# Column-tiled attention sums per 512-token block, table Gelu and Silu, and a hand-ordered interleave with the FFN matmuls

## The chip, the cores and the metric

One core of a Trainium2 chip; the rounds ran on different chips. The metric is the device time of one execution in microseconds, as a median over several executions; lower is better. A profile adds a span, from the first to the last instruction, which in the profiled runs here lies about 2 us below the time. Engines: PE is TensorE, DVE is VectorE, ACT is ScalarE, POOL is GpSimd, SP issues transfers. A "slot" is what one full 128x128x512 matmul takes in a stream.

## The reference

```python
x = A_x                                   # (1, 2048, 512) bf16
xn = layernorm(x)
q, k, v = split_heads(xn @ wqkv)          # 32 heads of 16
# each query attends to 8 keys, at distances 0, 2, ..., 14 back
logits = q . k[pos - 2*w] / 4             # w = 0..7, masked before the start
o = softmax(logits) @ v[pos - 2*w]
s = o @ wo
g = silu((gelu_tanh(xn @ w_gate) * (xn @ w_up)) @ w_down)   # 512 -> 1792 -> 512
return x + s * g
```

## The kernel before

Features lie on partitions, tokens along the free axis. A score is a product on DVE followed by a sum over the 16 features of each head, which PE does with a 0/1 matrix. The kernel runs stage after stage over all 2,048 tokens, and a scheduler chooses the order of instructions. The parts that matter here, cut:

```python
# scores: per window position w, per 128 features c, over all tokens
nc.vector.tensor_tensor(out=prodk[:], in0=q_sb[:, c, :],
                        in1=k_sb[:, c, koff : koff + S], op=ALU.mult)
for jq in range(NJ):
    o = 32 * jq + 8 * c
    nc.tensor.matmul(L_ps[:],                                  # all 128 rows
        lhsT=ind1[:, IND1_OFF - o : IND1_OFF - o + P],         # 128 columns, 8 not zero
        rhs=prodk[:, jq * TQ : (jq + 1) * TQ], ...)
# ... softmax over [128, 8, 512] at once, on DVE and ACT ...
# values: 128 products of 512 columns, each summed by a matmul with the identity
nc.vector.tensor_tensor(out=pv[:], in0=attn[:, w, :],
                        in1=v_arr[:, d, voff : voff + TQ], op=ALU.mult)
nc.tensor.matmul(oacc_ps[:], lhsT=ident[:], rhs=pv[:], start=(w == 0), stop=(w == W - 1))
# ...
# FFN, per 128 of the 1792 hidden features ("a pair": gate and up, 4 matmuls each)
nc.scalar.activation(out=u_bf[:], in_=u_ps[:], func=AF.Copy)
nc.scalar.activation(out=zt[:], in_=g_ps[:], func=AF.Square, scale=sqrt_c2)
nc.vector.scalar_tensor_tensor(out=zt[:], in0=zt[:], scalar=c1, in1=g_ps[:], op0=ALU.add, op1=ALU.mult)
nc.scalar.activation(out=zt[:], in_=zt[:], func=AF.Tanh)
nc.vector.scalar_tensor_tensor(out=gu[:], in0=g_ps[:], scalar=0.5, in1=u_bf[:], op0=ALU.mult, op1=ALU.mult)
heng.scalar_tensor_tensor(out=hT[:, fc, :], in0=zt[:], scalar=1.0, in1=gu[:], op0=ALU.add, op1=ALU.mult)
```

The softmax here doesn't subtract the row's maximum and nothing guards it: scores larger than these inputs give would overflow.

## Time and profile before

| | before |
|---|---|
| time, median of 3 runs | 321.88 us (320.28 to 322.45) |
| span of the profiled run | 319.8 us |
| busy PE / DVE / ACT | 287.3 / 245.1 / 165.8 us |
| full matmuls x slot | 1,184 x 0.2165 = 256.3 us |

One more view belongs beside them: the chain of waits, summed by engine. Its shares are of the span, and each part names what the end of the program was waiting on.

```profile
PE 48%; DVE 30%; ACT 17%; issue 2%; DMA 1%; DVEq 0%; ACTq 0%
```

Less than half of the end's path is PE's own work; 30% is DVE and 17% ACT.

### The profile page before, as it was taken

The page shows a single profiled execution, that of the slowest core. Times are in us where ns is not written, and L with a number is a line of the kernel's source. Part 1 is how long each engine was busy: PE and PEld are TensorE (multiplying, and loading weights), DVE is VectorE, ACT ScalarE, POOL GpSimd, SP SyncE. Part 2 cuts the span into 40 slices and gives each one's busy share as a digit, 9 for nine tenths or more (in the row PEclk, how much of TensorE's full clock was granted, in tenths as well). Part 3 has the DMA queues.
Part 4 walks back from the last instruction along what each step waited for, and adds up shares of the span by engine and source line. Part 5 has one row for each costly group of instructions (what it writes and reads, how often), then busy time and mean ns, then how long its engine had stood idle before and what let it go on. Part 6 is the DMA issues. An engine that isn't in the chain of part 4 may idle for free.

```text
span 319.8 us, 3547 instructions
## 1 busy us (share of the span) xinstructions
PE 287.3 (90%) x1248; PEld 119.6 (37%) x1248; DVE 245.1 (77%) x460; ACT 165.8 (52%) x281; POOL 1.4 (0%) x10
## 2 busy tenths in 40 slices
PE   0698999999998576999999999999999999999993
PEld 0444444444433222444332343344443334443341
DVE  4867710159999699989999999944389995899954
ACT  1155986642201835622222488827558882588811
POOL 1000000000000000000000000000000000000000
PEclk9999999999999956999999999999999999999998
DMA  7997111110000093000000197102410001200012
GB/s 248 395 371 235 66 35 33 67 66 0 2 0 0 1 214 56 1 0 0 2 0 1 28 198 240 61 0 68 132 53 14 2 0 36 87 10 1 0 35 66
DMA packets 17762, 22.57 MB, mean 71 GB/s; under 512 B 1104, under 2 KB 15696, under 8 KB 17744
## 3 DMA queue, kind: packets, MB, share of 16 engines
q1 hardware_dynamic: 17744, 22.34, 23.3%
q8 instruction: 10, 0.16, 0.2%
q14 instruction: 8, 0.07, 0.1%
HBM read 16.04 MB, written 6.29 MB: 70 GB/s over the span
## 4 chain that ended last, share of the span: by engine, by line
PE 48%; DVE 30%; ACT 17%; issue 2%; DMA 1%; DVEq 0%; ACTq 0%
DVE pv L275 13%; PE qkv_ps L181 13%; PE y_ps L358 13%; PE L_ps L223 7%; ACT zt L345 7%; DVE zt L342 7%; ACT zt L341 7%; PE g_ps L322 5%; PE s_ps L304 4%; PE u_ps L331 4%; DVE prodk L215 3%; DVE stats L142 1%; ACT u_bf L339 1%; PE tr_ps L162 1%; DVE hT L351 1%
## 5 line engine op out<-in xcount | busy, mean ns | idle before, releaser
L322 PE MATMUL g_ps<-xnT,wg_sb 128*128 128x512 bf16 x224 | 61.5, 391 | 8.1 <-ACT u_bf L339 2.8
L331 PE MATMUL u_ps<-xnT,wu_sb 128*128 128x512 bf16 x224 | 60.7, 390 | 6.2 <-ACT u_bf L339 3.9
L215 DVE TENSOR_TENSOR prodk<-q_sb,k_sb 128x2048 bf16<-128x2048 bf16 x32 | 37.5, 1222 | 25.0 <-ACT k_sb L196 21.0
L358 PE MATMUL y_ps<-wd_sb,hT 128*128 128x512 bf16 x224 | 55.3, 379 | 0.6
L181 PE MATMUL qkv_ps<-xnT,wqkv_sb 128*128 128x512 bf16 x192 | 43.7, 387 | 0.0
L275 DVE TENSOR_TENSOR pv<-attn,v_arr 128x512 bf16<-128x512 bf16 x128 | 43.0, 416 | 0.0
L342 DVE SCALAR_TENSOR_TENSOR zt<-zt,g_ps 128x512 bf16<-128x512 bf16 x56 | 38.3, 684 | 5.5 <-ACT zt L341 0.7
L345 ACT ACTIVATE zt<-zt 128x512 bf16<-128x512 bf16 x56 | 35.2, 629 | 12.0 <-DVE zt L342 11.6
L281 PE MATMUL oacc_ps<-pv,ident 128*128 128x512 bf16 x128 | 41.2, 378 | 0.0
L351 DVE SCALAR_TENSOR_TENSOR hT<-zt,gu 128x512 bf16<-128x512 bf16 x56 | 38.4, 686 | 3.5 <-ACT zt L345 2.8
L339 ACT ACTIVATE u_bf<-u_ps 128x512 bf16<-128x512 f32 x56 | 33.2, 593 | 14.1 <-PE u_ps L331 13.6
L341 ACT ACTIVATE zt<-g_ps 128x512 bf16<-128x512 f32 x56 | 33.1, 596 | 13.9 <-PE g_ps L322 7.8
L347 DVE SCALAR_TENSOR_TENSOR gu<-g_ps,u_bf 128x512 bf16<-128x512 f32 x56 | 38.3, 684 | 0.2 <-ACT u_bf L339 0.2
L322 PEld LDWEIGHTS <-wg_sb 128*128 128x128 bf16 x224 | 22.1, 99 | 42.6 <-issue 22.8
L331 PEld LDWEIGHTS <-wu_sb 128*128 128x128 bf16 x224 | 22.2, 100 | 33.2 <-issue 9.3
L223 PE MATMUL L_ps<-prodk,ind 128*128 128x512 bf16 x128 | 32.6, 378 | 1.7 <-DVE prodk L215 0.9
L358 PEld LDWEIGHTS <-hT 128*128 128x128 bf16 x224 | 21.5, 97 | 29.0 <-issue 3.3
L181 PEld LDWEIGHTS <-wqkv_sb 128*128 128x128 bf16 x192 | 18.9, 100 | 21.5 <-issue 0.2
L288 ACT ACTIVATE o_arr<-oacc_ps 128x512 bf16<-128x512 f32 x16 | 9.6, 597 | 33.2 <-PE oacc_ps L281 33.2
L367 DVE SCALAR_TENSOR_TENSOR g<-th,y_ps 128x512 bf16<-128x512 bf16 x16 | 10.9, 686 | 20.3 <-ACT th L366 20.3
L366 ACT ACTIVATE th<-y_ps 128x512 bf16<-128x512 f32 x16 | 9.5, 597 | 31.0 <-PE y_ps L358 30.7
L281 PEld LDWEIGHTS <-ident 128*128 128x128 bf16 x128 | 11.7, 96 | 23.3 <-issue 9.5
(41 smaller groups left out, 153.8 us busy)
## 6 DMA issues: line engine op xcount, KB each, us to landing
x_chunk<-in_A_x_dram SPq DMA_DIRECT2D x4, 512.0 KB, 4.8
x_t<-in_A_x_dram SPq DMA_DIRECT2D x16, 128.0 KB, 2.3
vT_dram<-vst SPq DMA_DIRECT2D x16, 128.0 KB, 1.8
oT_dram<-o_arr SPq DMA_DIRECT2D x4, 512.0 KB, 7.8
oT_fm<-oT_dram SPq DMA_DIRECT2D x4, 512.0 KB, 5.2
out_dram<-o_t SPq DMA_DIRECT2D x16, 128.0 KB, 1.7
wg_sb<-in_B_w_gate_dram SPq DMA_DIRECT2D x1, 1792.0 KB, 14.7
wu_sb<-in_B_w_up_dram SPq DMA_DIRECT2D x1, 1792.0 KB, 9.2
```

Source lines behind the costliest of these rows:

```text
L181: nc.tensor.matmul(ps[:], lhsT=wqkv_sb[:, dk, fo * P : (fo + 1) * P], rhs=xnT[:, dk, jq * TQ : (jq + 1) * TQ], start=(dk == 0), stop=(dk = ...
L215: nc.vector.tensor_tensor(out=prodk[:], in0=q_sb[:, c, :], in1=k_sb[:, c, koff : koff + S], op=ALU.mult,)
L223: nc.tensor.matmul(L_ps[:], lhsT=ind1[:, IND1_OFF - o : IND1_OFF - o + P], rhs=prodk[:, jq * TQ : (jq + 1) * TQ], start=(c == 0 and jq == ...
L275: nc.vector.tensor_tensor(out=pv[:], in0=attn[:, w, :], in1=v_arr[:, d, voff : voff + TQ], op=ALU.mult,)
L281: nc.tensor.matmul(oacc_ps[:], lhsT=ident[:], rhs=pv[:], start=(w == 0), stop=(w == W - 1),)
L322: nc.tensor.matmul(g_ps[:], lhsT=wg_sb[:, dk, fc * P : (fc + 1) * P], rhs=xnT[:, dk, jq * TQ : (jq + 1) * TQ], start=(dk == 0), stop=(dk = ...
L331: nc.tensor.matmul(u_ps[:], lhsT=wu_sb[:, dk, fc * P : (fc + 1) * P], rhs=xnT[:, dk, jq * TQ : (jq + 1) * TQ], start=(dk == 0), stop=(dk = ...
L341: nc.scalar.activation(out=zt[:], in_=g_ps[:], func=AF.Square, scale=sqrt_c2)
L342: nc.vector.scalar_tensor_tensor(out=zt[:], in0=zt[:], scalar=c1, in1=g_ps[:], op0=ALU.add, op1=ALU.mult)
L345: nc.scalar.activation(out=zt[:], in_=zt[:], func=AF.Tanh)
L351: heng.scalar_tensor_tensor(out=hT[:, fc, :], in0=zt[:], scalar=1.0, in1=gu[:], op0=ALU.add, op1=ALU.mult)
L358: nc.tensor.matmul(y_ps[:], lhsT=hT[:, fc, tt * P : (tt + 1) * P], rhs=wd_sb[:, fc, :], start=(fc == 0), stop=(fc == NF - 1),)
```

## The change

The intent has five parts.

1. Scores and values are worked block by block (512 tokens), with window position and head on the 128 partitions: 32 heads x 4 of the 8 window positions. One DVE product (128x2048) makes four window positions of the scores, or four features of the values, at a time.
2. The sums over features are column-tiled on PE: four matmuls with 32 output columns each, writing four different 32-partition strips of one bank, where the kernel before used full-width ones.
3. The softmax sums go to PE (fold and spread matrices); the reciprocal is taken on 128x128.
4. Gelu and Silu come from the activation tables: per pair one ACT and one DVE instruction in place of three and three.
5. The program order is kept on every engine (no scheduler). A small clock model in the generator decides where, among the QKV and FFN matmuls, each attention piece is put; a group's matmuls are released after the FFN pair at whose end its product should be ready.

Smaller things: x stays on chip, x block 0 comes as four 128 KB transfers with the QKV weights on a second queue, and the round trip of the attention output through memory goes.

The diff, cut to its core:

```diff
-    qkpool = ctx.enter_context(tc.tile_pool(name="qkpool", bufs=1))
-    pkpool = ctx.enter_context(tc.tile_pool(name="pkpool", bufs=2))
+    vpool = ctx.enter_context(tc.tile_pool(name="vpool", bufs=3))
+    prpool = ctx.enter_context(tc.tile_pool(name="prpool", bufs=3))
+    psf = ctx.enter_context(tc.tile_pool(name="psf", bufs=5, space=bass.MemoryType.PSUM))
+    psa = ctx.enter_context(tc.tile_pool(name="psa", bufs=3, space=bass.MemoryType.PSUM))
+
+    ctx.enter_context(tc.manual_schedule())
 ... (cut)
+    for t in range(TPB):
+        nc.sync.dma_start(out=x_sb[:, t, :], in_=x2d[t * P : (t + 1) * P, :])
+    for i in range(3):
+        nc.scalar.dma_start(
+            out=wqkv_sb[:, :, i * D : (i + 1) * D], in_=wqkv_v[:, :, i * D : (i + 1) * D]
+        )
 ... (cut)
                 nc.vector.tensor_tensor(
-                    out=prodk[:],
-                    in0=q_sb[:, c, :],
-                    in1=k_sb[:, c, koff : koff + S],
+                    out=prod[:],
+                    in0=st["q"][:, c, :].unsqueeze(1).to_broadcast([P, 4, TQ]),
+                    in1=kwin,
                     op=ALU.mult,
                 )
-                for jq in range(NJ):
-                    o = 32 * jq + 8 * c
-                    nc.tensor.matmul(
-                        L_ps[:],
-                        lhsT=ind1[:, IND1_OFF - o : IND1_OFF - o + P],
-                        rhs=prodk[:, jq * TQ : (jq + 1) * TQ],
-                        start=(c == 0 and jq == 0),
-                        stop=(c == NC - 1 and jq == NJ - 1),
-                    )
+                def reduce():
+                    if c == 0:
+                        st["L"] = psa.tile([P, TQ], F32, name="L_ps", tag="a")
+                    for w4 in range(4):
+                        nc.tensor.matmul(
+                            st["L"][32 * w4 : 32 * (w4 + 1), :],
+                            lhsT=ind[:, IOFF - 8 * c : IOFF - 8 * c + 32],
+                            rhs=prod[:, w4, :],
+                            start=(c == 0),
+                            stop=(c == NC - 1),
+                        )
 ... (cut: sums, spreading of the reciprocals)
-                nc.tensor.matmul(
-                    oacc_ps[:],
-                    lhsT=ident[:],
-                    rhs=pv[:],
-                    start=(w == 0),
-                    stop=(w == W - 1),
-                )
+                    for e in range(4):
+                        nc.tensor.matmul(
+                            st["O"][32 * e : 32 * (e + 1), :],
+                            lhsT=fold4[:, 0, :],
+                            rhs=pv[:, e, :],
+                            start=(w2 == 0),
+                            stop=(w2 == 1),
+                        )
 ... (cut)
-                nc.scalar.activation(out=u_bf[:], in_=u_ps[:], func=AF.Copy)
-                nc.scalar.activation(out=zt[:], in_=g_ps[:], func=AF.Square, scale=sqrt_c2)
-                (three DVE and one more ACT instruction, shown above)
+        nc.scalar.activation(out=gl[:], in_=g_ps[:], func=AF.Gelu_apprx_tanh)
+        nc.vector.tensor_tensor(out=hT[:, fc, :], in0=gl[:], in1=u_ps[:], op=ALU.mult)
 ... (cut)
+            vst = vpool.tile([P, TQ], BF16, name="vst")
+            nc.scalar.activation(out=vst[:], in_=ps[:], func=AF.Copy)
+            nc.sync.dma_start(out=vT_dram[c * P : (c + 1) * P, j * TQ : (j + 1) * TQ], in_=vst[:])
 ... (cut)
+    ln_stats(0)
+    for t in range(TPB):
+        ln_transpose(t, ln_norm(t))
 ... (cut)
+        for fc in range(NF):
+            ffn_pair(j, hT, fc)
+            pump_act(clk["pe"])
+            pump_pe(clk["pe"])
```

## The prediction

> **What bounds the kernel now.** I read, in this order: the busy shares and the forty slices, then stretches cut at the joints of the chain of waits, then the chain itself inside a stretch, then the costliest groups. The shares alone mislead, because a matmul's record is longer than its slot in the stream.
>
> From the page (busy shares, then slices):
>
> ```profile
> PE 287.3 (90%) x1248; PEld 119.6 (37%) x1248; DVE 245.1 (77%) x460; ACT 165.8 (52%) x281; POOL 1.4 (0%) x10
> ...
> DVE  4867710159999699989999999944389995899954
> ...
> PEclk9999999999999956999999999999999999999998
> ```
>
> PE is "90% busy", VectorE (DVE) 77%, with full DVE slices for most of the run and a dip of the granted clock in slices 14 and 15. To see what a matmul really costs I take runs without waits from the chain of waits (start, length, what):
>
> ```profile
> 38.51 29.45 PE qkv_ps L181 x136
> ...
> 137.37 43.02 DVE pv L275 x128
> ```
>
> 136 matmuls in 29.45 us are 0.2165 us each; that is the slot (the mean record is about 385 ns because the tail overlaps the next). The kernel before has 1,184 matmuls of 512 columns (224 x 3 for gate, up and down, 192 for QKV, 64 for the output projection, 128 + 128 in attention), so 256.3 us of 319.8. The rest is waiting or half clock. Where it is lost, by stretches (start:end length, busy us and count per engine, clock, DMA):
>
> ```profile
> 104.50:137.40 32.90, 24.73 (x86) 9.10 (x85) 28.77 (x48) 19.71 (x30) 0.00 (x0) 0.79 0.35 66
> 137.40:181.00 43.60, 43.42 (x164) 14.75 (x163) 43.60 (x131) 10.29 (x18) 0.00 (x0) 1.00 0.00 1
> 181.00:208.40 27.40, 26.06 (x112) 10.87 (x112) 25.24 (x40) 23.56 (x43) 0.00 (x0) 1.00 0.59 154
> ...
> 274.40:302.20 27.80, 26.03 (x112) 10.78 (x111) 25.42 (x41) 23.44 (x42) 0.00 (x0) 1.00 0.06 20
> ```
>
> In 104.5 to 137.4 (softmax) PE places 86 matmuls, 18.6 us of slots in 32.9. In 137.4 to 181 (attention times values) it places 164, 35.5 us in 43.6, although it reads as fully busy; DVE is at 100% there, so DVE sets that stage. Each gate/up stretch places 112, 24.2 us, in 27.4 to 27.8. There the chain runs in a ring outside PE:
>
> ```profile
> 285.77 0.70 DVE zt L342
> 286.47 0.02 issue
> 286.49 0.64 ACT zt L345
> 287.13 0.04 issue
> 287.18 0.61 ACT zt L341
> ```
>
> One ring is 2.04 us per gate/up pair against 8 slots = 1.73 us of PE. The polynomial-and-Tanh Gelu costs three of these DVE groups and three ACT groups per pair:
>
> ```profile
> L342 DVE SCALAR_TENSOR_TENSOR zt<-zt,g_ps 128x512 bf16<-128x512 bf16 x56 | 38.3, 684 | 5.5 <-ACT zt L341 0.7
> ...
> L351 DVE SCALAR_TENSOR_TENSOR hT<-zt,gu 128x512 bf16<-128x512 bf16 x56 | 38.4, 686 | 3.5 <-ACT zt L345 2.8
> ```
>
> The half clock of the softmax stretch, on PE's timeline:
>
> ```profile
> 113.33 1.86 PE L322 MATMUL g_ps<-xnT,wg_sb 128*128 128x512 bf16 x4 [0.69 <-ACT u_bf L339]
> ```
>
> Four matmuls take 1.86 us there against 1.02 at full clock: short waits are followed by a slower clock.
>
> So PE is the floor, and DVE, or the DVE-ACT ring, holds it off its floor in three of the stages.
>
> **What the Trainium skill says.** (1) "TensorE: Matmul & The Clock Gate", Part 3 on packing small matmuls: matmuls with 32 output columns in different column groups run at the same time; three of 512 columns measured 2.38x, and a pack spans one matmul plus about 4 ns per further tile. (2) "TensorEngine Tiling (Array Packing)", Key Properties: changing the tiling mode drains the engine. The kernel before has no column-tiled matmul, so its trace shows neither; these two make the widest part of my range. (3) "ScalarE: Activation LUTs", What ACT_TABLE_LOAD costs: about 1283 ns plus a drain, 2.66 us per switch. The trace agrees on 1283 ns but not on the rest: a load started at 28.56 and the activation after it at 29.85 us. I use 1.28. (4) "VectorE: DVE Perf Modes", side-by-side table: 2,048 bf16 elements at two per cycle take 1224 ns. The score products agree (1222 ns for 128x2048), and the normalisation with a broadcast operand (4,096 elements, 2280 ns) shows that broadcasting keeps that rate.
>
> **The change part by part.**
> PE. Removed: the 256 full-width matmuls of attention, 256 x 0.2165 = 55.4 us. Added in their place: 64 groups of four column-tiled matmuls, all four in one bank on different 32-partition strips. Lower bound, if four run as one and nothing drains: 0.22 us a group. Upper bound, with a drain on both sides: record minus slot is 378 - 216 = 0.16 us, so 0.22 + 0.16 + 0.16 = 0.54. I choose the middle, 0.38: 64 x 0.38 = 24.3 us, an estimate. The sums and the spreading of the reciprocals by PE: eight column-tiled and four full 128-column matmuls per block, which I put at 0.6 us, four times, 2.4. Kept: 928 full matmuls, 200.9 us, and the transposes (a set of four at full clock went from 16.55 to 16.78, so 0.25 us; twelve sets inside the stream, 3.0).
>
> DVE. Gelu falls from three operations a pair to one: 112 x 0.685 = 76.7 us gone. Value products go from 128 of 512 columns at a pitch of 0.336 (43.0 / 128) to 32 of 2,048 at 1.22: 43.0 to 39.1. The softmax sums leave DVE; the reciprocal falls from 512 columns to 4 x 128, the same elements. The whole: LayerNorm 25.7 + small 0.7, products 64 x 1.222 = 78.2, hT 56 x 0.684 = 38.3, end of tile 16 x (0.69 + 0.42) = 17.8, reciprocals and casts 4.2, normalising 2.5, together about 167 us against 245. That is below PE.
>
> ACT. 148 activations of 128x512 at 0.60 = 88.8, four small ones 1.2, and 19 table loads in the instruction order (4 before) x 1.283 = 24.4: 114 against 166.
>
> DMA. The oT round trip through memory goes; v is read back four times over (4 x 2.1 MB), but for each block a long time before its use. x stays on chip, so 16 reloads go. None of it lies on the path.
>
> The path that sets the end, stage by stage:
> - Start to the first QKV matmul: before it is 13.2 us, with eight tiles' statistics in front. Now the first 128 KB of x land after some 2.3 us (as x_t did), four statistics at a pitch of 0.66, root and reciprocal, then four rounds of normalise, transpose, copy at about 1.5 us each (12.31 to 13.83 in the trace): 3.1 + 3.0 + 0.6 + 6.0 = 12.7. Hardly a gain.
> - Half clock at the start: before, until about 16.8 us, some 3.5 us; costs 1.7.
> - Stream: 200.9 + 3.0 + 24.3 + 2.4 = 230.6.
> - Waits inside the stream: 4, an estimate. In the QKV stage both in-order engines meet at each transpose; in the FFN stage an Exp between Gelus holds ACT for 1.28 + 0.6 + 1.28 = 3.2 us, but five PSUM banks let PE go on for four groups, 3.5 us, so most is hidden.
> - Tail: Silu 0.6, two DVE operations 1.1, then output DMA to the end as before (317.05 to 319.8, 2.75), with gaps 4.6.
> Sum: 12.7 + 1.7 + 230.6 + 4.0 + 4.6 = 253.6. Of the 66 us saved, 29 are PE work (55.4 - 26.7), the other 37 are waits and half clock: 14 in the softmax stretch, 8 in the value stretch, 10 in three gate/up stretches, the rest scattered.
>
> **The rivals.**
> A: column tiles do not overlap. Then 256 x 0.2165 = 55.4 come back, 31 us more: about 285. Against it: page (1), and the four outputs lie on different partition strips. Still faster than before.
> B: the drain is full and weight loads are exposed as well: 0.54 to 0.65 a group, 10 to 17 us more: 264 to 271.
> C: DVE becomes the bound in the gate/up stage. A pair there has one product and one hT, 1.22 + 0.68 = 1.90 us against 1.73 + 0.38 = 2.11 of PE. Close, so if the groups are as cheap as 0.22 (1.95), DVE and PE nearly tie and the saving of cheap groups comes back as short waits. This limits the gain downwards to about 243.
> D: table loads. Fifteen of the 19 surround four Exps or change between Gelu and Silu after the FFN begins; if each Exp exposed its 3.2 us, 13 more: about 263.
> E: the hand order is made for guessed durations; if an engine arrives late at a meeting, in-order queues pass the wait on. Before, the scheduler's order lost 37 us; I cannot see more than about 10 here.
>
> **Range and chances.** Predicted 254 us. Cheap groups and no waits give about 241 (254 - 10 - 3); rival B or D gives 264 to 270. I take 242 to 268. Faster by over 2% (below 315) would fail only if several rivals came together with the half clock: 0.97; within 2% 0.02; slower 0.01.
>
> **What would show it.** PE slots: QKV, gate, up and down still at 0.2165 us. A group of four column-tiled matmuls at 0.3 to 0.45 from its first start to the next full matmul; 0.22 means no drain, over 0.8 means rival A. DVE busy near 167 and ACT near 114 us. Granted clock 1.0 after the start, without the dip. The chain of waits nearly all PE; long DVE or ACT pieces in it would be C or D. First QKV matmul near 12.7 us. The prediction is wrong if PE stands still for more than 10 us in the stream, or if the clock falls again.

## The result, and the profile after

| | before | after |
|---|---|---|
| time, median of 4 runs | 322.16 us (320.28 to 322.78) | 260.35 us (259.37 to 261.26) |
| span / mean granted clock | 319.8 us / 0.974 | 259.1 us / 0.993 |

The ratio is 0.8094, with a 95% interval of 0.8058 to 0.813. Ratios here are the mean time of one kernel's fast runs over the mean of the other's fast runs of the same rounds, so they are not quite the ratio of the medians that are quoted. "Before" in all later rounds had a median of 322.5 us. The four executions of the kernel after had mean clocks of 0.993, 0.992, 0.996 and 1.000 and took 260.82, 261.26, 259.88 and 259.37 us.

First the page of the kernel after: busy shares, the slices of DVE and of the granted clock, and the summary of the chain of waits.

```profile
PE 236.5 (91%) x1271; PEld 98.9 (38%) x1296; DVE 160.5 (62%) x233; ACT 110.9 (43%) x171; POOL 5.8 (2%) x33
...
DVE  2573878468978886998988972149844133443231
...
PEclk9999999989999999999999999999999999999999
...
PE 82%; issue 8%; DVE 4%; DMA 2%; ACT 2%; SPq 0%; POOL 0%; POOLq 0%; ACTq 0%
```

PE went from 48% of the chain to 82%; DVE from 30% to 4%, ACT from 17% to 2%. The long dip of the clock is gone. One slice with an 8 is left (slice 9 of 40, some 52 to 58 us, just behind a stop at 50 us that is taken up below). DVE's 160.5 us and ACT's 110.9 answer to the predicted 167 and 114.

The stage of the FFN, as a stretch (start:end length, then busy us and count of PE, weight loads, DVE, ACT and POOL, granted clock, DMA share, GB/s):

```profile
76.40:254.68 178.28, 176.72 (x929) 74.14 (x944) 108.91 (x139) 74.26 (x110) 0.00 (x0) 1.00 0.17 37
```

The clock is 1.00 and PE is busy for 176.72 of 178.28 us, with DVE at 108.91. All waits of PE in the kernel after are those before its first transposes and QKV matmuls, a few in the QKV stage, and 0.7 us of short ones later: in the FFN stage PE waits for no other engine. So the ring of 2.04 us per pair is gone. At the end of the program pairs stand at 219.08, 219.94 and 220.81 us, 0.866 per four matmuls, which is four slots of 0.2165.

A change of table, on the timeline at the first pairs of the last block:

```profile
215.58 1.28 ACT L429 ACT_TABLE_LOAD   x1
...
216.87 1.28 ACT L429 ACTIVATE gl<-g_ps 128x512 bf16<-128x512 f32 x2
```

The load takes 1.28 us and the activation starts 0.01 us behind it. PE does not notice: its gate groups on both sides start at 214.76 and 216.49, 1.73 us apart, as without a load. It goes on into the next banks.

Now the three places that cost more than predicted. The start, on DVE's timeline:

```profile
5.57 0.69 DVE L189 BATCH_NORM_STATS2 stats<-x_sb 128x6 f32<-128x512 bf16 x1 [1.22 <-DMA x_sb<-in_A_x_dram]
...
7.59 0.69 DVE L189 BATCH_NORM_STATS2 stats<-x_sb 128x6 f32<-128x512 bf16 x1 [1.11 <-DMA x_sb<-in_A_x_dram]
```

The first tile is there at 3.44 us, and the others do not come behind it at DVE's pace: the second and the third tile keep it waiting for another 1.22 and 1.11 us. PE then:

```profile
15.82 6.54 PE L387 MATMUL qkv_ps<-xnT,wqkv_sb 128*128 128x512 bf16 x20 [0.52 <-DVE xnT L215]
22.19 0.39 PE L214 MATMUL tr_ps<-ident,xn_t 128*128 128x128 bf16 x4
```

The first QKV matmul is at 15.82 us, not 12.7. Twenty of them take 22.19 - 15.82 = 6.37 us until the next transposes, against 20 x 0.2165 = 4.33: 2.0 us of half clock. The clock's row of the page shows 9 in these slices all the same, so half clock at the start is read from the pace of the matmuls. The set of transposes behind them has a record of 0.39; the set ahead, at half clock, had 0.61.

A column group in the stream:

```profile
61.34 1.04 PE L387 MATMUL qkv_ps<-xnT,wqkv_sb 128*128 128x512 bf16 x4
62.31 0.40 PE L248 MATMUL L_ps<-prod,ind 128*32 128x512 bf16 x4
62.64 1.04 PE L387 MATMUL qkv_ps<-xnT,wqkv_sb 128*128 128x512 bf16 x3
```

From 61.34 to 62.64 are 1.30 us; four full matmuls take 0.866 of it, so the group costs 0.43. Worked out in this way for 35 lone groups of the trace, the mean is 0.426 us (0.414 to 0.434). The four matmuls are one record of 0.40 us, hardly longer than a single matmul's 0.38: they do run together.

And the stop in the QKV stage, on the timeline of all engines:

```profile
46.99 0.60 ACT L406 ACTIVATE vst<-qkv_ps 128x512 bf16<-128x512 f32 x1 [2.72 <-DMA vT_dram<-vst]
...
49.72 0.18 DVE L195 RECIPROCAL rstd<-rstd 128x4 f32<-128x4 f32 x1 [2.65 <-ACT rstd L192]
...
50.40 0.40 PE L214 MATMUL tr_ps<-ident,xn_t 128*128 128x128 bf16 x4 [1.74 <-DVE xn_t L200]
```

ACT can't copy the last piece of V of a block before one of three vst buffers (they hold V on its way to memory) is free, and that comes with the landing of an earlier store. ACT is in order, so the root for the next LayerNorm waits behind it, to 49.39 us; DVE waits for the root (2.65 us), PE for the normalised tile (1.74 us), and after that pause PE runs eight QKV matmuls at half clock: 50.63 to 53.93, 3.30 us in place of 1.73. The half clock does not follow such a stop each time: the group-pairs run below has the same stop and goes on at full clock.

### The profile page after: what moved, and what is told of

Read it like the earlier page. It is cut to its first block, busy times and chain, and to the rows that moved or that the text cites. A ratio compares the mean times of both kernels' runs of the same rounds, so it can differ in the third digit from the quotient of the medians.

```text
span 259.1 us, 3296 instructions
## 1 busy us (share of the span) xinstructions
PE 236.5 (91%) x1271; PEld 98.9 (38%) x1296; DVE 160.5 (62%) x233; ACT 110.9 (43%) x171; POOL 5.8 (2%) x33
## 4 chain that ended last, share of the span: by engine, by line
PE 82%; issue 8%; DVE 4%; DMA 2%; ACT 2%; SPq 0%; POOL 0%; POOLq 0%; ACTq 0%
PE g_ps L420 19%; PE y_ps L462 19%; PE u_ps L433 18%; PE qkv_ps L387 12%; PE s_ps L452 5%; PE O_ps L339 4%; PE L_ps L248 3%; DMA x_sb<-in_A_x_dram 2%; PE tr_ps L214 2%; DVE prod L237 1%; DVE xnT L215 1%; DVE xn_t L200 1%; DVE stats L189 1%; ACT L429 0%; ACT sil L472 0%
## 5 line engine op out<-in xcount | busy, mean ns | idle before, releaser
L443 DVE TENSOR_TENSOR hT<-gl,u_ps 128x512 bf16<-128x512 bf16 x56 | 38.4, 686 | 31.5 <-PE u_ps L433 24.4
L429 ACT ACTIVATE gl<-g_ps 128x512 bf16<-128x512 f32 x56 | 33.3, 597 | 48.2 <-PE g_ps L420 46.8
L237 DVE TENSOR_TENSOR prod<-q_sb,k_sb 128x2048 bf16<-128x2048 bf16 x32 | 38.5, 1218 | 1.0 <-PE O_ps L339 0.8
L328 DVE TENSOR_TENSOR pv<-attn,v_arr 128x2048 bf16<-128x2048 bf16 x32 | 38.7, 1220 | 0.7 <-PE O_ps L339 0.5
L476 DVE TENSOR_TENSOR sg<-sil,s_ps 128x512 bf16<-128x512 bf16 x16 | 11.0, 686 | 36.3 <-ACT sil L472 36.3
L472 ACT ACTIVATE sil<-y_ps 128x512 bf16<-128x512 f32 x16 | 9.6, 597 | 48.9 <-PE y_ps L462 45.6
L420 PEld LDWEIGHTS <-wg_sb 128*128 128x128 bf16 x224 | 19.0, 98 | 25.7 <-issue 7.7
L452 PE MATMUL s_ps<-wo_sb,o_sb 128*128 128x512 bf16 x60 | 15.9, 380 | 0.3 <-issue 0.2
L189 DVE BATCH_NORM_STATS2 stats<-x_sb 128x6 f32<-128x512 bf16 x16 | 10.8, 672 | 4.8 <-DMA x_sb<-in_A_x_dram 4.8
L401 ACT ACTIVATE k_sb<-qkv_ps 128x512 bf16<-128x512 f32 x16 | 9.6, 598 | 7.9 <-PE qkv_ps L387 6.0
L248 PE MATMUL L_ps<-prod,ind 128*32 128x512 bf16 x128 | 12.4, 389 | 0.1
```

What stands on the lines that cost most here:

```text
L189: nc.vector.bn_stats(out=stats[:, t, :], in_=x_sb[:, t, :])
L237: nc.vector.tensor_tensor(out=prod[:], in0=st["q"][:, c, :].unsqueeze(1).to_broadcast([P, 4, TQ]), in1=kwin, op=ALU.mult,)
L248: nc.tensor.matmul(st["L"][32 * w4 : 32 * (w4 + 1), :], lhsT=ind[:, IOFF - 8 * c : IOFF - 8 * c + 32], rhs=prod[:, w4, :], start=(c == 0), ...
L328: nc.vector.tensor_tensor(out=pv[:], in0=st["attn"][:, w2, :].unsqueeze(1).to_broadcast([P, 4, TQ]), in1=st["v"][:, 4 * g : 4 * (g + 1), 8 ...
L420: nc.tensor.matmul(g_ps[:], lhsT=wg_sb[:, dk, fc * P : (fc + 1) * P], rhs=xnT[:, dk, j * TQ : (j + 1) * TQ], start=(dk == 0), stop=(dk == ...
L429: nc.scalar.activation(out=gl[:], in_=g_ps[:], func=AF.Gelu_apprx_tanh)
```

## The experiments

All kernels gave a correct result. Theory: the gain comes from three separable things, taking DVE and ACT out of the way (tables), column tiles that run as one matmul, and an order that feeds PE all the time; of the miss, the start, the lone groups and the V stores are the terms. Rival: the four matmuls of a group only look parallel, or the order matters little, or the lost microseconds lie elsewhere and come back when these are removed.

### Column tiling undone in the kernel after

```diff
-                            st["L"][32 * w4 : 32 * (w4 + 1), :],
-                            lhsT=ind[:, IOFF - 8 * c : IOFF - 8 * c + 32],
+                            st["L"][:],
+                            lhsT=indw[:, 120 - 32 * w4 - 8 * c : 248 - 32 * w4 - 8 * c],
-                            start=(c == 0),
-                            stop=(c == NC - 1),
+                            start=(c == 0 and w4 == 0),
+                            stop=(c == NC - 1 and w4 == 3),
 (the same for the values, with foldw)
```

> The changed kernel with the column tiling of the attention sums undone: the same 256 products are summed by full-width matmuls (128 output columns, zeros outside the wanted 32). Theory (PE is the bound, and four column-tiled matmuls run as one): a lone group took 0.43 us from the last full matmul's slot to the next in the trace of the changed kernel, four full matmuls take 4 x 0.2165 = 0.87, and groups that follow each other directly go from 0.22 to 0.87; over 64 groups 28 to 32 us more: 288 to 292 us, with the clock at 1.0. Rival (the groups lie beside waits that DVE or ACT set, so PE work is partly free): 262 to 275 us.

Measured: 286.09 us (285.75 to 287.19), ratio 0.8877. PE's timeline of this kernel:

```profile
63.11 1.03 PE L254 MATMUL L_ps<-prod,indw 128*128 128x512 bf16 x3
63.98 1.03 PE L393 MATMUL qkv_ps<-xnT,wqkv_sb 128*128 128x512 bf16 x4
```

A group now takes 63.98 - 63.11 = 0.87 us, four slots (one of its four records is missing from the trace). The tiling is worth 286.09 - 260.35 = 25.7 us in this kernel, a little under the 64 x (0.866 - 0.426) = 28 of its groups: the slower PE gives the V stores time, and ACT waits for them only 2.5 us here against 8.2, so the stop of PE is not there. The rival range of 262 to 275 is out, and so is rival A of the prediction.

### Column tiling alone, in the kernel before

```diff
-                    o = 32 * jq + 8 * c
-                        L_ps[:],
-                        lhsT=ind1[:, IND1_OFF - o : IND1_OFF - o + P],
-                        start=(c == 0 and jq == 0),
-                        stop=(c == NC - 1 and jq == NJ - 1),
+                        L_ps[32 * jq : 32 * (jq + 1), :],
+                        lhsT=ind1[:, IND1_OFF - 8 * c : IND1_OFF - 8 * c + 32],
+                        start=(c == 0),
+                        stop=(c == NC - 1),
```

> The kernel before with another part alone: the 128 score sums as 32 groups of four column-tiled matmuls into the four strips of the same bank. It takes 128 x 0.2165 - 32 x 0.43 = 14 us from PE. Theory (DVE is full in the score stretch, 68 to 104.5 us, and sets it): the time stays within 1%, 318 to 323 us. Rival (PE work always counts, as PE is 90% busy): 306 to 310 us.

Measured: 321.47 us (321.35 to 323.36), ratio 0.9981 (0.995 to 1.0013): the same. Its timeline of PE:

```profile
86.42 0.62 PE L222 MATMUL L_ps<-prodk,ind 128*32 128x512 bf16 x4 [0.52 <-DVE prodk L215]
87.56 0.62 PE L222 MATMUL L_ps<-prodk,ind 128*32 128x512 bf16 x4 [0.52 <-DVE prodk L215]
```

and that of the kernel before in the same stage:

```profile
87.12 1.02 PE L223 MATMUL L_ps<-prodk,ind 128*128 128x512 bf16 x4
...
88.26 1.02 PE L223 MATMUL L_ps<-prodk,ind 128*128 128x512 bf16 x4
```

The pitch is one DVE product, 1.14 us in both. What PE no longer does is idle time, and the clock falls to half in it (0.62 for a group that takes 0.40 earlier in the same stage). The first value product comes only 1.3 us earlier (136.11 against 137.37 us) where PE had some 14 us less to do, and the time stays the same within its interval. Tiling of scores and values is worth 25.7 us where PE is fed; tiling of the scores, half of it, is worth nothing where DVE sets the pace.

### Table Gelu and Silu alone, in the kernel before

```diff
-                u_bf, Square, multiply-add, Tanh, two products (six instructions, shown above)
+                gl = fpool.tile([P, TQ], BF16, name="gl")
+                nc.scalar.activation(out=gl[:], in_=g_ps[:], func=AF.Gelu_apprx_tanh)
+                nc.vector.tensor_tensor(out=hT[:, fc, :], in0=gl[:], in1=u_ps[:], op=ALU.mult)
-                th = Tanh(0.5 * y_ps); g2 = (th + 1) * y_ps
+                nc.scalar.activation(out=g2[:, t, :], in_=y_ps[:], func=AF.Silu)
```

> The kernel before with one part of the change alone: Gelu and Silu from the tables, everything else as before. Theory (the ring of DVE and ACT holds the gate/up stretches, DVE fills the softmax stretch): three gate/up stretches fall from 27.5 to about 24.5 us, the tail by 0.7, the softmax stretch by some 5: 300 to 308 us. Rival (attention on DVE sets the time and the gate/up work only fills it): over 314 us.

Measured: 303.65 us (303.44 to 303.67), ratio 0.9414, inside the theory's range. Its page, busy shares and DVE slices:

```profile
PE 277.0 (92%) x1225; PEld 119.4 (40%) x1248; DVE 163.4 (54%) x332; ACT 115.4 (38%) x178; POOL 1.4 (0%) x10
...
DVE  4967300149999669409999974310534333234322
```

DVE falls from 245.1 to 163.4 us and its slices after the value stage from mostly 9 to 0 to 5. The stretches that stay full (slices 10 to 13 and 19 to 23) are the score and value products: these the tables do not touch. So of the 62 us some 19 are the tables' own. With the full-width run above the rest falls into two: from 303.65 to 286.09, 17.6 us, for the blocks, the softmax on PE and the interleave; from 286.09 to 260.35, 25.7 us, for the column tiles. This split holds in this order only, since the parts depend on each other, and how the 17.6 us divide among blocks, softmax and interleave was not tested.

### The scheduler's order in the kernel after

```diff
-    ctx.enter_context(tc.manual_schedule())
```

> The changed kernel without the manual schedule: the same instructions and buffers, ordered by the scheduler. Theory (the hand order is a real part of the gain, because in the scheduler's order many products stand in front of one hT and groups gather in front of few FFN matmuls, so PE waits for DVE): 270 to 285 us, PE starved and DVE full in some slices. Rival (the gain comes from less work on DVE and PE, order is secondary): 257 to 265 us.

Measured: 266.81 us (266.42 to 267.22), ratio 0.8277: 6.5 us more than by hand, between the two ranges. The view of PE's waits (us in total, times, longest):

```profile
PE g_ps L419 <- DVE hT L442: 2.3, 5, 0.8
```

With 1.7 each for a copy of K, a Gelu and a score product and 0.8 for a reciprocal these sum to 8.2 us, and none of them is in the kernel after. The scheduler puts attention's products ahead of the hT (Gelu times up) that frees an FFN bank. The hand order is worth some 6 us on balance, so most of the gain is in the operations. By stages it is not better everywhere: from the first gate matmul to PE's last the scheduler's order takes 185.6 us against 178.2, but from the first QKV matmul to the first gate matmul it takes 57.3 against 60.6; PE has no stop at the V stores there, and the clock is 1.00.

### More buffers for the V stores

```diff
-    vpool = ctx.enter_context(tc.tile_pool(name="vpool", bufs=3))
+    vpool = ctx.enter_context(tc.tile_pool(name="vpool", bufs=8))
```

> The changed kernel with eight staging buffers for V instead of three. Theory (near 45 us in the trace ACT waits 2.7 us for a V store that is queued behind the reads of v, its root for the next LayerNorm comes late, DVE waits 2.65 us for it and PE 1.74 us, after which eight matmuls run at half clock, 3.5 us in place of 1.7): this chain goes, 3 to 5 us less: 255 to 257 us, no half clock near 50 us. Rival (the wait only moves to the next thing that needs a DMA or to ACT's table load): over 259 us.

Measured: 257.83 us (257.52 to 257.99), ratio 0.8014: 2.5 us less, between the two ranges. PE's timeline where the stop had been:

```profile
49.05 1.89 PE L387 MATMUL qkv_ps<-xnT,wqkv_sb 128*128 128x512 bf16 x8
51.19 0.40 PE L214 MATMUL tr_ps<-ident,xn_t 128*128 128x128 bf16 x4 [0.25 <-DVE xn_t L200]
```

The eight matmuls are a record of 1.89 in place of 3.51 us, and the wait of 1.74 is not there. One buffer count was the cause of that stop. Its whole cost in the trace, some 3.7 us with the half clock and slow transposes behind it, is more than the 2.5 us of the medians: one of the four executions of the kernel after had a clock of 1.000 throughout, and in this run the first twenty QKV matmuls took 6.96 us against 6.37.

### x block 0 ahead of the QKV weights

```diff
-    for t in range(TPB):
-        nc.sync.dma_start(out=x_sb[:, t, :], in_=x2d[t * P : (t + 1) * P, :])
+    nc.sync.dma_start(
+        out=x_sb[:, 0:TPB, :], in_=x2d[0:TQ, :].rearrange("(t p) d -> p t d", p=P)
+    )
-        nc.scalar.dma_start(          # the three parts of wqkv
+        nc.sync.dma_start(
```

> The changed kernel with x's first block as one transfer and the QKV weights behind it on the same queue, as the kernel before has it. Theory (the four small transfers share the engines with 1.5 MB of weights, so the third lands at 7.5 us; alone the block lands near 4.4 us as before): first QKV matmul at about 12.8 instead of 15.8 us, total 3 us less: 256 to 258 us. Rival (the weights then come too late for the first QKV matmuls, or the time is lost again later): over 259 us.

Measured: 260.82 us (260.32 to 261.49), ratio 0.8103: no gain, as the rival had it. PE's timeline:

```profile
14.08 4.28 PE L388 MATMUL qkv_ps<-xnT,wqkv_sb 128*128 128x512 bf16 x13 [0.51 <-DVE xnT L216]
...
48.46 1.02 PE L388 MATMUL qkv_ps<-xnT,wqkv_sb 128*128 128x512 bf16 x4 [1.53 <-ACT vst L407]
```

The first QKV matmul is 1.74 us earlier (14.08 us; the theory had 12.8): all 512 KB have landed at 4.3 us and DVE no longer waits between tiles. The run changed the splitting of x and the order of the queues at once, so it does not say which of them did it. But PE stops twice in the QKV stage for a vst (1.30 us at 32.86 and 1.53 at 48.46): an earlier start brings V to the same three buffers earlier. The wait of 1.74 us with half clock behind it is in this run too. The gain was turned into another wait.

### Both together

The edits of the last two experiments.

> The changed kernel with eight V buffers and x's first block ahead of the weights, both. Theory (the 1.7 us that the earlier x won at the start were lost again at the V stores, which end at a fixed time because the weights are ahead of them on the queue; with the V buffers nothing waits there): the start's 1.8 us now reach the end: 257.8 - 1.8 = 256.0 us. Rival (the early x is swallowed by something else): 257.4 us or more.

Measured, 6 runs: 255.53 us (255.06 to 256.4), ratio 0.7945. With the buffers there, the earlier x reaches the end: 2.3 us less than with the buffers alone, where it had been worth nothing by itself. This settles the reading of the failed run before.

### Column groups in pairs

The matmuls of a group are released only after every second FFN pair, so that two groups stand side by side; a fourth product buffer holds the one that waits. A first form, which let an Exp see the bank of the following sums, read the bank before its sums were done and was mended before anything ran.

```diff
-    prpool = ctx.enter_context(tc.tile_pool(name="prpool", bufs=3))
+    prpool = ctx.enter_context(tc.tile_pool(name="prpool", bufs=4))
-                        act_q.append((clk["pe"] + 0.2, 0.6, expo))
+                        act_q.append((clk["pe"] + 0.2, 0.6, lambda L=st["L"]: expo(L)))
-            pump_pe(clk["pe"])
+            if fc % 2 == 1:
+                pump_pe(clk["pe"])
```

> The changed kernel with the column-tiled groups of the FFN stage taken in pairs (after every second gate/up pair), one more product buffer. Theory (0.22 of the 0.43 us of a lone group is the change between full and column-tiled mode, a following group costs 0.22 as in the three that stand together at 120.4 us in the trace): 15 changes fewer, 3 us less: 256 to 258 us, a pair of groups at 0.65 us. Rival (the groups wait for DVE, or the later softmax sums delay the values): 259 us or more.

Measured: 256.48 us (256.3 to 258.24), ratio 0.7986: 3.9 us less. PE's timeline:

```profile
81.81 1.03 PE L433 MATMUL u_ps<-xnT,wu_sb 128*128 128x512 bf16 x4
82.76 0.62 PE L339 MATMUL O_ps<-pv,fold 128*32 128x512 bf16 x8
83.31 1.04 PE L420 MATMUL g_ps<-xnT,wg_sb 128*128 128x512 bf16 x4
```

Two groups cost 83.31 - 81.81 - 0.866 = 0.63 us (14 pairs of the trace: mean 0.639) against 0.426 for one. A second group next to the first costs 0.213, one slot; so the change of mode there and back is worth another 0.21. By program order 56 groups stand alone in the kernel after and 26 in this one, 16 pairs having been made of the others: with one more change saved in each of some 15 pairs, about 3.2 us, an estimate from these numbers; 3.9 were measured. The traces show where the rest lies. From the first gate matmul to PE's last are 174.9 us against 178.2, 3.3 less, as estimated; the first gate matmul is at 75.10 against 76.40 us, and that part lies ahead of the stage in which the edit regroups matmuls:

```profile
50.35 0.40 PE L214 MATMUL tr_ps<-ident,xn_t 128*128 128x128 bf16 x4 [1.74 <-DVE xn_t L200]
50.58 1.89 PE L387 MATMUL qkv_ps<-xnT,wqkv_sb 128*128 128x512 bf16 x8
```

The stop at the V stores is here as well, with the same wait, but the eight matmuls behind it run at full clock (1.89 us, not 3.51), and the first twenty QKV matmuls happened to take 5.44 us, not 6.37.

### Matmuls of zeros before the first transposes

```diff
+    for i in range(NWARM):      # 28, from 1.45 us
+        nc.tensor.matmul(w_ps[:], lhsT=ident[:], rhs=warm[:], start=(i == 0), stop=(i == NWARM - 1))
```

> The changed kernel with 28 matmuls on zeros before the first transpose, results unread. Theory (the first twenty QKV matmuls took 6.54 us where 4.33 is their slot; work beforehand raises the granted clock): 2.2 us less, near 258 us, the twenty in about 4.5 us. Rival (the clock falls again in the gaps between the transposes, or matmuls on zeros do not count): unchanged, 260 us.

Measured: 261.68 us (260.52 to 261.77), ratio 0.8127: no gain. PE's timeline:

```profile
10.80 0.40 PE L215 MATMUL tr_ps<-ident,xn_t 128*128 128x128 bf16 x4 [1.46 <-DVE xn_t L201]
12.04 0.61 PE L215 MATMUL tr_ps<-ident,xn_t 128*128 128x128 bf16 x4 [0.84 <-DVE xn_t L201]
...
16.05 5.68 PE L388 MATMUL qkv_ps<-xnT,wqkv_sb 128*128 128x512 bf16 x20 [0.52 <-DVE xnT L216]
```

The zeros ran from 1.45 to 9.34 us. The first set of transposes is at full clock (0.40), the second at half (0.61), and so are most of the first QKV matmuls. Fillers that end before a sparse stretch do not carry over it. The twenty QKV matmuls take 5.52 us here, from 16.05 to the next transposes at 21.57, against 6.37 in the kernel after, but this can't be put down to the zeros: in the eight runs without fillers whose QKV stage is built this way the twenty took from 5.44 to 6.96 us. PE also waits 1.7 us for a vst here.

### The findings put together

Five vst buffers, x first, groups in pairs, and the normalisation of the next tile placed ahead of the copy of this one, all in one kernel:

```diff
+    xn = [ln_norm(0), ln_norm(1)]
     for t in range(TPB):
-        ln_transpose(t, ln_norm(t))
+        ln_transpose(t, xn[t])
+        if t + 2 < TPB:
+            xn.append(ln_norm(t + 2))
```

> Five V buffers, x first, groups in pairs, and in the first block the normalisation of the next tile issued before the copy of this one. Theory (the parts are independent): 260.4 - 2.5 - 1.8 - 3.9 = 252.2, and 1.5 to 2 us less from the shorter start: 250 to 252 us, first QKV matmul near 12.4 us. Rival (parts overlap, the half clock that pairs happened to avoid counts twice): 252.5 to 254.

Measured, 6 runs: 250.21 us (250.03 to 251.06), ratio 0.7782. On PE's timeline the first QKV matmul is at 12.04 us, but the half clock stays: the record of twenty is 6.35 us long, against 6.54 in the kernel after.

### The same with fillers between the transposes

22 matmuls of zeros before the transposes and two after each set.

> As the combined version, with 22 matmuls on zeros before the first transposes and two after each set of four transposes, so that PE has no long gap before QKV. Theory (the warm-up alone failed because the clock fell in the gaps of 0.84 us between the transposes): the first twenty QKV matmuls take about 4.5 us instead of 5.6 to 7.1, 1 to 2.5 us less than the combined version. Rival (matmuls on zeros do not raise or hold the clock): the same as the combined version within 0.5 us.

Measured, 6 runs: 252.03 us (251.76 to 252.99), ratio 0.784: slower by 1.8 us, a miss of both. PE's timeline says why:

```profile
5.99 7.26 PE L492 MATMUL w_ps<-warm,ident 128*128 128x512 bf16 x22 [5.99 <-POOL warm L487]
...
15.95 4.48 PE L389 MATMUL qkv_ps<-xnT,wqkv_sb 128*128 128x512 bf16 x20
```

The fillers do what was hoped for: the record of the twenty QKV matmuls is 4.48 us, full clock (4.31 to the next transposes, outside the 5.44 to 6.96 without fillers). But the tile of zeros was written by GpSimd behind its other work, so the fillers began at 5.99 us and held PE until 13.08, and the first QKV matmul slid from 12.04 to 15.95. That is 3.9 lost and 1.9 won.

### The fillers begun earlier

```diff
-    nc.gpsimd.memset(warm[:], 0.0)      # after the other constants
-    dummy(22); then dummy(2) after each transpose set
+    nc.vector.memset(warm[:], 0.0)      # first of all on DVE
+    dummy(25); then dummy(3) after the second set, dummy(2) after the last
```

> The best version so far (250.2 us) with 25 matmuls of zeros from the earliest moment (the tile of zeros is now written by VectorE first of all, not last by GpSimd), three more between the second and third transpose set and two before the first QKV matmul. In the run with 22 fillers that began at 5.99 us the first twenty QKV matmuls took 4.48 us (full clock) instead of 6.35, but the fillers held PE until 13.08 and the first QKV matmul slid from 12.04 to 15.95. Theory (both effects add, and the slide was only the late start of the fillers): first QKV near 12.1 us, twenty in about 4.5 us, total 250.2 - 1.8 = 248.4 us (247.8 to 249.2). Rival (the idle 0.4 to 0.5 us that stay between transposes bring the half clock back, as in the run with 28 fillers before the transposes alone): twenty QKV in 5.6 us or more, total 249.6 to 251.

Measured, 5 runs: 248.69 us (248.17 to 248.72), ratio 0.772: 1.5 us less than without fillers, within the theory's range. PE's timeline:

```profile
10.77 0.40 PE L216 MATMUL tr_ps<-ident,xn_t 128*128 128x128 bf16 x4 [0.26 <-DVE xn_t L202]
...
11.68 4.48 PE L389 MATMUL qkv_ps<-xnT,wqkv_sb 128*128 128x512 bf16 x19
```

QKV starts at 11.68 us and at full clock (one of its twenty records is missing); the transposes ahead of it are at full clock too (0.40). This is the fastest version found, 11.7 us under the kernel after.

## Why the prediction was right

The time fell inside the range of 242 to 268, 6.35 us above the 254 that was named. By its own steps:

| term | predicted, us | measured, us |
|---|---|---|
| to the first QKV matmul | 12.7 | 15.8 |
| half clock at the start | 1.7 | 2.0 |
| full matmuls and transposes | 203.9 | 203.7 (928 x 0.2165 and twelve sets at 0.23) |
| 64 column groups | 24.3 | 26.2 (56 x 0.426, one pair 0.64, two threes 0.85 each) |
| softmax sums and spreading | 2.4 | about 3.1 (0.57 + 0.22 a block, read in the full-width run) |
| waits in the stream | 4.0 | about 4.7 (listed below) |
| tail | 4.6 | 4.4 |
| sum / span | 253.6 | 259.9 / 259.1 |

The measured terms come from single places of the trace and overshoot the span by 0.8. Of the 6.35 us, 5.5 are in the span. The rest is that the sum was of a span and was called a time: in the profiled run the time, 260.82, lies 1.7 above the span (the median is 0.5 under that run, and 254 is the sum rounded up by 0.4). The terms erred nearly all to one side, so nothing large cancelled. The half clock at the start is luck in part: with 5.44 to 6.96 us for the twenty matmuls it costs 1.1 to 2.6 us from run to run.

Of the readings and sums, three are off without bearing on the result: the dip of the clock stands in slices 15 and 16, counted from one; 16.55 to 16.78 are 0.23 us, not 0.25; and rival D's 13 us on 254 give 267, not 263 (263 follows only if the 4 us of waits are taken off first).

**The floor and what held PE off it** was right. PE's slot stayed at 0.2165 us, DVE and ACT fell to 160.5 and 110.9 us against 167 and 114, and PE alone sets the FFN stage. The table-only run and the tiles-only run show the same from the side of the kernel before: there DVE set the pace, and less PE work bought nothing.

**The start** was the largest mis-sized term, 3.1 us. The rounds of normalise, transpose and copy were right (9.88 to 15.82 are 5.94 us, 6.0 predicted). What went wrong is "four statistics at a pitch of 0.66" behind a first tile at some 2.3 to 3.1 us: the fourth statistic ended at 9.1, most likely because the small x transfers shared the engines with the QKV weights on the second queue. The Trainium skill, "DMA: Bandwidth & Descriptors", section "Issuing engines are not separate DMA queues", says that transfers from different engines run on the same 16 DMA engines and interleave; the x-first run agrees, with all four tiles there at 4.28 us (still 1.2 us later than the 3.1 that was put), though it also made the four transfers one.

**The group's cost** was put at 0.38 and is 0.426 us, in the 0.3 to 0.45 that was named as the sign of being right. The reasoning behind the bounds holds too: the change of mode costs 0.21 us a group in total, not 0.16 on both sides. Rival B (0.54 and more) is out by the direct reading, rival A by the full-width run.

**The waits** were put at 4 and came to about 4.7: 1.74 and 0.17 at the V stores, 1.6 for half clock after them and 0.2 for slow transposes, 0.5 before the softmax sums, 0.5 at two transposes. The size was near, but not the place: "None of it lies on the path", said of the transfers, does not hold for the V stores, which the list there leaves out and which held ACT for 8.2 us in all. And one sign that was named for being wrong did come, "if the clock falls again": it fell to half for 3.4 us after that stop, at 1.8 us of cost. The other, 10 us of standing still, did not. That the two in-order engines would meet badly at the transposes (rival E) is what did happen; that a store would be the one to come late was not foreseen.

**Rivals C and D** did not come: in the FFN stage PE waits for no other engine, DVE has 108.91 busy us in 178.28, and table loads are passed over by PE. Rival C remains untested for still cheaper groups; at 26 lone groups the time still fell.

What stays open: why the same stop of 1.74 us is followed by half clock in one execution (the kernel after, the x-first run) and not in another (the group-pairs run), and what the parts of the 17.6 us are worth.

## What to carry to other kernels

Before taking work off the engine that reads as busiest, ask of each stage who ends the waits: column tiling was worth 25.7 us where PE was fed, and the half of it that the scores are was worth nothing where DVE set the pace. An engine that is in order passes the wait for one buffer on to everything queued behind it, so count the buffers of a store against its landing time, and expect a gain at the start to stop there until they suffice. Put matmuls of one tiling mode side by side, since each change there and back costs as much as the group itself (0.21 us each here). And before a fraction of a microsecond in one trace is put down to an edit, look how much the same place varies in runs that the edit can't have touched: the first twenty QKV matmuls differed by 1.5 us.

## What the Trainium skill lacked or had wrong

- "ScalarE: Activation LUTs", "What ACT_TABLE_LOAD costs": a switch is given as 2.66 us with the drain. In both kernels the load took 1.28 us and the activation started at once behind it: 28.56 to 29.85 before, 215.58 to 216.87 after.
- "TensorEngine Tiling (Array Packing)", "Key Properties": the drain at a change of mode has no number. Here it costs about 0.21 us for going to 32-column tiles and back (0.426 us for a lone group, 0.639 for two in a row).
- "TensorE: Matmul & The Clock Gate", Part 3: there is no measured figure for four column tiles of 512 columns (its table has three). Inside a row of groups such a four costs 0.213 us, one slot of a full matmul, so it is 4 times as fast as four full ones; alone, with the change of mode, 0.426 against 0.866, 2.0 times.
- The same page, "Why this matters for your kernels": it asks for no idle gaps above some 3 us to keep the clock; its Part 1 does tell of short idle times between groups of matmuls that let the clock swing, but gives no length. Here five gaps of 0.73 to 0.74 us between groups of four column-tiled matmuls came before half clock (0.40 us records growing to 0.62 in the tiles-only run). A stop of 1.74 us was followed by eight matmuls in 3.30 us instead of 1.73 in one run, and by full clock in another. Its Part 4 says that transposes do not count as busy; the zeros run (full clock lost within 2.7 us of the last filler, with one set of transposes between) and the last run (three fillers between the sets kept it) do not contradict that, but they don't separate the transposes from the idle time around them.
- "DMA: Bandwidth & Descriptors": it says that queues share the engines, but not what that does to a small first transfer. Four 128 KB tiles beside three weight transfers on a second queue gave DVE the third tile at 7.59 us; one 512 KB transfer with the weights behind it on the same queue gave all of them at 4.28 us.
